# Computing a per-token gate with row sums on VectorE instead of column-tiled matmuls on the matrix engine

## The chip, the cores and the metric

The kernel runs on one core of one Trainium2 chip. The metric is device time in microseconds (us). PE is the matrix engine and PEld its weight loads, DVE is VectorE, ACT is ScalarE, POOL is GpSimd, SP is SyncE, which issues nearly all DMA transfers. The profile covers one execution of the core. Its span is about 1.8 us shorter than the device time of the same execution.

## The reference, cut to what matters

Two attention blocks, A (linear attention) and B (a sliding window of 8 dilated positions), read the same `x` of 2048 tokens by 1024 features. A gate mixes their results:

```python
g = sigmoid((x * gate_w).sum(-1, keepdims=True))      # one number per token
return g * A(x) + (1 - g) * B(x)
```

Most of the projections are 1728 matmuls of 128x128 by 512 columns. The gate is one dot product of 1024 terms for each of 2048 tokens.

## The kernel before: the parts that matter

The kernel is written as a list of operations, each with an engine, an estimated cost, what it reads and writes, and a rank (`prio`, lower goes first). A list scheduler in the kernel, called the planner below, orders each engine's instructions from that. An eviction (the copy of a finished sum out of an accumulator) may have the engine `"any"`; the planner then gives it to ScalarE or VectorE, whichever it expects to be done first. The list fixes the order in which each engine gets its instructions, and SyncE its transfers. An eviction is the copy of a finished sum out of an accumulator.

The first stage computes block B's values, and `x` comes in through transposing loads. The gate stands right behind it, then the keys and queries of B follow:

```python
gwr = SB([128, 8, 32], BF16, "gwr")              # gate_w, 32 copies of each column
P.op("dve", lambda e: e.tensor_copy(gwr[...], gw[:, :, None].to_broadcast([128, 8, 32])), ...)
gbank = main.next()
def gate_fn(e):
    for dc in range(8):
        for u in range(4):                       # four column tiles of 32
            last = e.matmul(gbank.ap()[32 * u:32 * u + 32, :], gwr[:, dc, :], xT[:, dc, u * 512:(u + 1) * 512],
                            start=(dc == 0), stop=(dc == 7), tile_position=(0, 32 * u), skip_group_check=True)
    return last
P.op("pe", gate_fn, 1.75, mode="c", reads=[gwr.all(), xT.all()], writes=[gbank.iv], name="gate")
P.op("act", lambda e: e.activation(gts[:, :], gbank.ap(), ACT.Exp, scale=-1.0), ...)
P.op("sp", ... gt_hbm <- gts[0:128:32, :] ...)   # to DRAM, to turn a row of tokens into partitions
P.op("sp", ... gt <- gt_hbm, rearranged ...)     # and back
# then on VectorE, 128x16 each: gt + 1, g = 1 / gt, gm = 1 - g
...
WARM = 9     # matmuls on zeros at the very start, before data is there
```

Of the kernel before, what the change touches and what calls it, by code (L numbers as in the profile page):

```python
# [6 lines left out]
ACT = mybir.ActivationFunctionType  # L7
ALU = mybir.AluOpType
AX = mybir.AxisListType
BF16 = mybir.dt.bfloat16  # L10
F32 = mybir.dt.float32
I32 = mybir.dt.int32

D = 1024
# [1088 lines left out]
def build_kernel(nc, A_x, A_wqkv, A_wo, B_x, B_wqkv, B_wo, gate_w, out):  # L1103
    del B_x
    S = A_x.shape[1]
    NT = S // 128
    HS = S // 2
    x2 = A_x[0].rearrange("(m e) d -> e m d", e=2)
# [5 lines left out]
    def SB(shape, dtype, name, at=None):  # L1114
        n = SZ[dtype]
        for d in shape[1:]:
            n *= d
        if at is None:
            at = base[0]
            base[0] += (n + 31) // 32 * 32  # L1120
        uid[0] += 1
        h = nc.alloc_sbuf_tensor_at("%s_%d" % (name, uid[0]), list(shape), dtype, offset=at)
        return Tile("S", h, at, list(shape), dtype)
# [29 lines left out]
    vB_hbm = nc.dram_tensor("vB_hbm", [S, D], BF16)  # L1153
    MX = [("M", 0, 1, None)]
    mx_hbm = nc.dram_tensor("mx_hbm", [4, 128], F32)
    GT = [("M", 1, 2, None)]
    gt_hbm = nc.dram_tensor("gt_hbm", [4, 512], F32)

    def hb(p0, p1, half):
        return [("H%d" % half, p0, p1, None)]  # L1160

    xT = SB([128, 8, S], BF16, "xT")
# [8 lines left out]
    KINDS = ((57, (0, 7)), (57, (7, 7)), (56, (7, 8)))  # L1171
    msk = [SB([128, 2, n], BF16, "msk%d" % i) for i, (n, _) in enumerate(KINDS)]
    eps = SB([128, 1], F32, "eps")
    gw = SB([128, 8], BF16, "gw")
    gt = SB([128, NT], F32, "gt")
    g = SB([128, NT], F32, "g")
    gm = SB([128, NT], F32, "gm")
    gwr = SB([128, 8, 32], BF16, "gwr")
    kvbd = SB([128, 8, 128], BF16, "kvbd")
    zbd = SB([128, 8, 128], BF16, "zbd")  # L1180
    kva = SB([128, 8, 33], F32, "kva")
# [5 lines left out]

    ph = base[0]
    vst = Ring([SB([128, 512], BF16, "vst%d" % i) for i in range(8)])
    gts = SB([128, 512], F32, "gts", at=ph)  # L1190
    top_ = base[0]
    base[0] = ph
    Er = Ring([SB([128, 32 * 57], BF16, "E%d" % i) for i in range(2)])
# [8 lines left out]
    ph = base[0]  # L1202
    mx = [SB([128, 1024], BF16, "mx%d" % i, at=ph + 2048 * i) for i in range(2)]
    pk = Ring([SB([128, 1024], BF16, "pk%d" % i) for i in range(2)])
    az = Ring([SB([128, H, 33], BF16, "az%d" % i) for i in range(2)])
    top_ = base[0]
    base[0] = ph
    osb = Ring([SB([128, 1024], BF16, "o%d" % i) for i in range(2)])
# [11 lines left out]
    act = lambda n: 0.19 + n / 1200.0  # L1220
    dps = lambda n: 0.14 + n / 960.0

    def plan(seen):

        P = Prog(nc, nc.alloc_semaphore)
# [66 lines left out]
        def load_x(t, prio):  # L1292
            e_, r = t // 8, t % 8
            return P.op("sp", lambda e: e.dma_start_transpose(xT[:, :, t * 128:(t + 1) * 128], x2[e_, r * 128:(r + 1) * 128, :]),  # L1294
                        1.5, writes=[xT.part((0, 8), (t * 128, (t + 1) * 128))], prio=prio, chan="x%d" % t, lat=1.3)

        def load_w(slot, half, src, c0, prio, d0=0, d1=8, eng="sp", after=()):
            n = d1 - d0
            return P.op(eng, lambda e: e.dma_start(ws[slot][:, d0:d1, half * 512:half * 512 + 512], src[:, d0:d1, c0:c0 + 512]), 0.4 + 0.2 * n,  # L1299
                        writes=[ws[slot].part((d0, d1), (half * 512, half * 512 + 512))], prio=prio, chan="w%d_%d_%d" % (slot, half, d0), lat=0.55 * n, after=after)  # L1300

        def gw_load(e):
            with nc.allow_non_contiguous_dma(reason="tiny gate_w transposed load"):
                return e.dma_start(gw[:, :], gate_w.rearrange("(dc p) -> p dc", p=128))

        load_x(0, 0)
        load_w(0, 0, Bw, 2048, 0.1, 0, 2, "act")
        load_w(0, 0, Bw, 2048, 0.2, 2, 4, "act")
# [3 lines left out]
            load_x(t, 3 + t)  # L1312
        for d in range(0, 8, 2):
            load_w(0, 1, Bw, 2560, 6.1 + 0.1 * d, d, d + 2)
        P.op("sp", gw_load, 0.6, writes=[gw.all()], prio=20, chan="gw", lat=0.5)


        main = Pool(banks[0:7])
# [49 lines left out]
        for t, half in [(4 * b + i, half) for b in range(NT // 4) for half in range(2) for i in range(4)]:  # L1368
# [5 lines left out]
            for d in range(0, 8, step):  # L1374
# [3 lines left out]
                 writes=[hb(t * 128, (t + 1) * 128, half)], chan="vst%d" % vs, lat=0.5, prio=5)  # L1378
# [3 lines left out]
        load_w(0, 1, Aw, 2560, 31)  # L1382


        P.op("dve", lambda e: e.tensor_copy(gwr[:, :, :], gw[:, :, None].to_broadcast([128, 8, 32])), 0.3, reads=[gw.all()], writes=[gwr.all()])
        gbank = main.next()

        def gate_fn(e):
            last = None
            for dc in range(8):  # L1390
                for u in range(4):
                    last = e.matmul(gbank.ap()[32 * u:32 * u + 32, :], gwr[:, dc, :], xT[:, dc, u * 512:(u + 1) * 512], start=(dc == 0), stop=(dc == 7),  # L1392
                                    tile_position=(0, 32 * u), skip_group_check=True)
            return last
        P.op("pe", gate_fn, 1.75, mode="c", reads=[gwr.all(), xT.all()], writes=[gbank.iv], name="gate")
        P.op("act", lambda e: e.activation(gts[:, :], gbank.ap(), ACT.Exp, scale=-1.0), act(512), reads=[gbank.iv], writes=[gts.all()])
        P.op("sp", lambda e: e.dma_start(gt_hbm[:, :], gts[0:128:32, :]), 0.6, reads=[gts.all()], writes=[GT], chan="gto", lat=1.0)

        def gate_in(e):
            with nc.allow_non_contiguous_dma(reason="2048 gates"):  # L1400
                return e.dma_start(gt[:, :], gt_hbm.rearrange("u (k p) -> p (u k)", p=128))
        P.op("sp", gate_in, 0.6, reads=[GT], writes=[gt.all()], chan="gti", lat=6.0)
        P.op("dve", lambda e: e.tensor_scalar(gt[:, :], gt[:, :], 1.0, None, op0=ALU.add), 0.1, reads=[gt.all()], writes=[gt.all()], prio=1e5)
        P.op("dve", lambda e: e.reciprocal(g[:, :], gt[:, :]), 0.25, reads=[gt.all()], writes=[g.all()], prio=1e5)
        P.op("dve", lambda e: e.tensor_scalar(gm[:, :], g[:, :], -1.0, 1.0, op0=ALU.mult, op1=ALU.add), 0.1, reads=[g.all()], writes=[gm.all()], prio=1e5)
# [3 lines left out]
        main = Pool(banks[0:4])  # L1409
# [146 lines left out]
        main = Pool(banks)  # L1556
# [109 lines left out]
        for t in range(NT):  # L1666
# [4 lines left out]
            for f0, f1 in parts:  # L1671
# [3 lines left out]
                def fn(e, t=t, bank=bank, f0=f0, f1=f1):  # L1675
# [6 lines left out]
                    out=o_[:, i0 * 128:i1 * 128].rearrange("p (i s) -> p i s", s=128), in0=bank.ap(0, n).rearrange("p (i s) -> p i s", s=128),  # L1682
                    scalar=gm[:, t:t + 1], in1=tgt[:, i0:i1, c0:c0 + 128], op0=ALU.mult, op1=ALU.add), dps(n),
                    reads=[bank.iv, gm.all(), tgt.part((i0, i1), (c0, c0 + 128))], writes=[o_.part((f0, f1))])
                if t == NT - 1 or f1 == 1024:
                    c = f0 if t == NT - 1 else 0
                    P.op("sp", lambda e, e_=e_, r=r, o_=o_, c=c, f1=f1: e.dma_start(out2[e_, r * 128:(r + 1) * 128, c:f1], o_[:, c:f1]), 0.5,
                         reads=[o_.part((c, f1))], chan="out%d_%d" % (os_, c), lat=1.0)
# [8 lines left out]
    for _ in range(PASSES):  # L1697
        got = plan(seen)
        seen = got[2]
        if best is None or got[0].span < best[0].span:  # L1700
            best = got
    P, flag_op = best[:2]
# [22 lines left out]
def bass_gated_mix__linear_attn_block__sliding_local_dilated__prompt_kernel(nc, A_x, A_wqkv, A_wo, B_x, B_wqkv, B_wo, gate_w, out):  # L1725
    return build_kernel(nc, A_x, A_wqkv, A_wo, B_x, B_wqkv, B_wo, gate_w, out)
# [28 lines left out]
```

## Time and profile before

| | before |
|---|---|
| time, median of 3 runs | 504.89 us (504.59 to 505.67) |
| PE busy | 97% of the span |
| VectorE busy | 53% |
| ScalarE busy | 38% |
| gate matmuls on the chain of waits | 1.84 us |

The page's first part gives busy time (share of the span) and number of instructions for each engine:

```profile
PE 488.5 (97%) x5190; PEld 232.6 (46%) x5257; DVE 264.6 (53%) x456; ACT 192.9 (38%) x335; POOL 6.6 (1%) x30
```

PE is the bottleneck.

The chain of waits, read in order of time: start, duration, what.

```profile
58.71 3.40 PE ps_all L1324 x15
62.11 1.84 PE ps_all L1392 x32
63.95 0.54 PE ps_all L1324 x2
...
127.95 0.63 PE ps_all L1427 x64
...
498.26 0.48 DVE o L1681
```

L1392 is the gate. It is a link of the chain, with other matmuls right ahead of it and right behind it. L1427 is the first group of attention scores, at 127.95 us. The last line is VectorE's last operation. The matmuls around the gate, from the timeline of PE:

```profile
62.05 1.91 PE L1392 MATMUL ps_all<-xT,gwr 128*32 128x512 bf16 x32
63.89 11.40 PE L1324 MATMUL ps_all<-xT,w 128*128 128x512 bf16 x51
```

The gate begins at 62.05 us and the next group at 63.89: 1.84 us.

What the new operations could cost can be read from similar ones. Groups by form on VectorE: names, partitions x elements and types, count, then busy us, mean ns of one.

```profile
L1436 DVE TENSOR_TENSOR E<-E,msk 128x1824 bf16<-128x1824 bf16 x16 | 17.6, 1102 | 13.7 <-ACT E L1433 13.7
L1681 DVE SCALAR_TENSOR_TENSOR o<-ps_all,gm,xT 128x512 bf16<-128x512 f32 x23 | 17.3, 750 | 22.5 <-PE ps_all L1677 22.5
L1681 DVE SCALAR_TENSOR_TENSOR o<-ps_all,gm,xT 128x256 bf16<-128x256 f32 x2 | 1.0, 483 | 0.5 <-PE ps_all L1677 0.4
```

Whether they have room depends on the stretch. The stretches view: length, then busy us (and instructions) of PE, PEld, DVE, ACT and POOL, granted PE clock, DMA share, GB/s.

```profile
52.00:60.00 8.00, 7.95 (x37) 3.61 (x37) 1.87 (x3) 1.19 (x2) 0.00 (x0) 1.00 1.08 345
68.00:76.00 8.00, 7.95 (x38) 3.63 (x38) 4.70 (x8) 1.34 (x3) 0.00 (x0) 1.00 0.78 186
76.00:84.00 8.00, 8.00 (x39) 3.64 (x38) 4.77 (x8) 1.19 (x2) 0.00 (x0) 1.00 0.01 1
100.00:108.00 8.00, 7.95 (x38) 3.64 (x38) 4.89 (x8) 1.19 (x2) 0.00 (x0) 1.00 0.00 0
```

VectorE works under 2 of 8 us from 36 to 60 us, and 3.8 to 5.0 of 8 us while keys and queries are computed. The DMA engines are full until about 72 us and idle afterwards.

### The profile page before, as it was taken

Reading aid. Unit: us, or ns where it says so; the run is one execution under the profiler, and the core shown is the slowest. Engines: PE = TensorE matmul, PEld = TensorE weight load, DVE = VectorE, ACT = ScalarE, POOL = GpSimd, SP = SyncE. Lnnn points to the kernel's source line nnn. Section 1 sums busy time; section 2 is a strip of 40 time slices with the busy share of each in tenths; the row PEclk is TensorE's granted clock in tenths of the full one; section 3 lists DMA queues with packets and bytes.
Section 4 is the critical chain, followed back from the end, with each engine's and each line's share of the span. In section 5 each row is a group of like instructions: output and inputs, shape, how many; then the busy total and the mean of one; then the engine's idle time right before and its main releaser. Section 6 shows DMA issues by size and latency. Waiting matters only on the chain.

```text
span 502.5 us, 11582 instructions
## 1 busy us (share of the span) xinstructions
PE 488.5 (97%) x5190; PEld 232.6 (46%) x5257; DVE 264.6 (53%) x456; ACT 192.9 (38%) x335; POOL 6.6 (1%) x30
## 2 busy tenths in 40 slices
PE   8999999999999999999999999999999999999996
PEld 2444444444454444544544545444444444444443
DVE  3112235556667676454555464678776563234443
ACT  1111111111354454655554555479864543100000
POOL 5000000000000000000000000000000000000000
PEclk9999999999999999999999999999999999999999
DMA  8999990000024060100010100500000000011222
GB/s 222 207 204 314 353 270 1 1 0 1 12 86 139 22 198 27 34 23 23 23 39 21 33 1 3 170 0 1 0 2 0 2 0 1 1 43 64 83 78 73
DMA packets 47410, 34.92 MB, mean 69 GB/s; under 512 B 22261, under 2 KB 43125, under 8 KB 47354
## 3 DMA queue, kind: packets, MB, share of 16 engines
q1 hardware_dynamic: 46810, 33.59, 23.6%
q8 instruction: 43, 0.70, 0.6%
q10 hardware_dynamic: 544, 0.52, 0.4%
q14 instruction: 13, 0.11, 0.1%
HBM read 21.51 MB, written 8.40 MB: 60 GB/s over the span
## 4 chain that ended last, share of the span: by engine, by line
PE 95%; issue 2%; DMA 1%; ACT 1%; SPq 0%; DVE 0%
PE ps_all L1324 76%; PE ps_all L1677 11%; PE ps_all L1427 2%; PE ps_all L1447 2%; PE ps_all L1602 1%; PE ps_all L1452 1%; PE ps_all L1523 1%; DMA xT<-in_A_x_dram 1%; PE ps_all L1580 1%; ACT ra L1604 0%; PE ps_all L1392 0%; SPq L1294 0%; SPq L1299 0%; ACT e L1333 0%; ACT ra L1605 0%
## 5 line engine op out<-in xcount | busy, mean ns | idle before, releaser
L1324 PE MATMUL ps_all<-w,xT 128*128 128x512 bf16 x922 | 207.8, 379 | 5.6 <-issue 4.0
L1324 PE MATMUL ps_all<-xT,w 128*128 128x512 bf16 x747 | 169.2, 379 | 2.5 <-issue 1.9
L1324 PEld LDWEIGHTS ps_all<-w,xT 128*128 128x128 bf16 x960 | 91.3, 98 | 110.3 <-issue 1.7
L1324 PEld LDWEIGHTS ps_all<-xT,w 128*128 128x128 bf16 x768 | 73.9, 98 | 88.8 <-ACT ra L1604 0.6
L1677 PE MATMUL ps_all<-w,qT 128*128 128x512 bf16 (+1 forms) x259 | 55.2, 373 | 0.3
L1677 PEld LDWEIGHTS ps_all<-w,qT 128*128 128x128 bf16 x264 | 25.8, 98 | 29.7
L1335 DVE TENSOR_SCALAR e<-e 128x512 bf16<-128x512 bf16 x64 | 18.4, 291 | 38.9 <-ACT e L1331 25.3
L1355 DVE CAST vst<-ps_all 128x512 bf16<-128x512 f32 x15 | 10.4, 691 | 42.7 <-PE ps_all L1324 42.7
L1433 ACT ACTIVATE E<-ps_all 128x1824 bf16<-128x1824 f32 (+1 forms) x18 | 30.4, 1687 | 3.1 <-PE ps_all L1427 2.0
L1331 ACT ACTIVATE e<-ps_all 128x512 bf16<-128x512 f32 x32 | 19.1, 597 | 31.6 <-PE ps_all L1324 30.8
L1333 ACT ACTIVATE e<-ps_all 128x512 bf16<-128x512 f32 x32 | 19.2, 601 | 29.3 <-PE ps_all L1324 27.8
L1681 DVE SCALAR_TENSOR_TENSOR o<-ps_all,gm,xT 128x512 bf16<-128x512 f32 (+1 forms) x25 | 18.2, 729 | 23.0 <-PE ps_all L1677 22.8
L1280 DVE TENSOR_TENSOR mx<-mx,kT 128x1024 bf16<-128x1024 bf16 x32 | 20.7, 688 | 16.9 <-ACT kT L1356 16.8
L1280 DVE TENSOR_TENSOR mx<-mx,qT 128x1024 bf16<-128x1024 bf16 x32 | 20.7, 688 | 16.7 <-ACT qT L1359 16.6
L1356 ACT ACTIVATE vst<-ps_all 128x512 bf16<-128x512 f32 x17 | 10.1, 597 | 47.8 <-PE ps_all L1324 47.8
L1436 DVE TENSOR_TENSOR E<-E,msk 128x1824 bf16<-128x1824 bf16 (+1 forms) x18 | 19.8, 1100 | 14.5 <-ACT E L1433 14.5
L1462 DVE TENSOR_TENSOR qT<-ps_all,L 128x456 bf16<-128x456 f32 (+1 forms) x36 | 21.1, 624 | 7.7 <-ACT L L1461 7.7
L1359 ACT ACTIVATE qT<-ps_all 128x512 bf16<-128x512 f32 x15 | 9.0, 597 | 37.0 <-PE ps_all L1324 37.0
L1337 DVE SCALAR_TENSOR_TENSOR pk<-ps_all,e 128x512 bf16<-128x512 f32 x32 | 22.0, 688 | 0.8
L1604 ACT ACTIVATE ra<-ps_all,eps 128x512 f32<-128x512 f32 x32 | 21.5, 688 | 2.2 <-PE ps_all L1602 2.0
L1356 ACT ACTIVATE az<-ps_all 128x512 bf16<-128x512 f32 x19 | 11.4, 600 | 27.6 <-PE ps_all L1324 27.6
L1356 ACT ACTIVATE kT<-ps_all 128x512 bf16<-128x512 f32 x14 | 8.4, 597 | 35.5 <-PE ps_all L1324 35.5
(77 smaller groups left out, 336.5 us busy)
## 6 DMA issues: line engine op xcount, KB each, us to landing
w<-in_A_wqkv_dram SPq DMA_DIRECT2D x6, 1024.0 KB, 8.2
v<-vB_hbm SPq DMA_DIRECT2D x36, 128.0 KB, 2.6
vB_hbm<-vst SPq DMA_DIRECT2D x32, 128.0 KB, 4.9
w<-in_B_wqkv_dram SPq DMA_DIRECT2D x4, 1024.0 KB, 8.3
out_dram<-o SPq DMA_DIRECT2D x15, 256.0 KB, 2.0
w<-in_A_wo_dram SPq DMA_DIRECT2D x2, 1024.0 KB, 5.6
w<-in_B_wo_dram SPq DMA_DIRECT2D x2, 1024.0 KB, 6.5
w<-in_B_wqkv_dram SPq DMA_DIRECT2D x6, 256.0 KB, 4.1
```

The costliest lines, as they stand in the source:

```text
L1280: P.op("dve", lambda e, m=m, op=op: e.tensor_tensor(m[:, 0:n], m[:, 0:n], src, op), 0.08 + n / 1920.0, reads=[m.all(), reg], writes=[m.all()],
L1324: last = e.matmul(bank.ap(), lhs(dc), rhs(dc), start=(dc == 0), stop=(dc == 7))
L1331: P.op("act", lambda e: e.activation(e_[:, :], bank.ap(), ACT.Exp), act(512), reads=[bank.iv], writes=[e_.all()])
L1333: P.op("act", lambda e: e.activation(e_[:, :], bank.ap(), ACT.Exp, accum_out=qe[:, col:col + 1]), act(512) + 0.1, reads=[bank.iv], writes= ...
L1335: P.op("dve", lambda e: e.tensor_scalar(e_[:, :], e_[:, :], 1.0, 1e-6, op0=ALU.min, op1=ALU.add), 0.25, reads=[e_.all()], writes=[e_.all()])
L1337: P.op("dve", lambda e: e.scalar_tensor_tensor(out=dst, in0=bank.ap(), scalar=0.0, in1=e_[:, :], op0=ALU.max, op1=ALU.add), dps(512), read ...
L1356: fa = lambda e: e.activation(dst, src(), ACT.Copy)
L1433: P.op("act", lambda e: e.activation(E[:, 0:32 * nq].rearrange("p (j q) -> p j q", j=4), ps[:, 4:8, 0:8 * nq], ACT.Exp), act(32 * nq), rea ...
L1436: P.op("dve", lambda e: e.tensor_tensor(ev(), ev(), m[:, :, :].rearrange("p r q -> p (r q)")[:, None, :].to_broadcast([128, 16, 2 * nq]), ...
L1462: P.op("dve", lambda e, L=L, pb=pb, g=g: e.tensor_tensor(qT[:, 4 * g:4 * g + 4, t0 + qs:t0 + qs + 2 * nq].rearrange("p c (h q) -> p h c q" ...
L1604: P.op("act", lambda e: e.activation(R[:, :], db.ap(), ACT.Ln, bias=eps[:, :]), act(512), reads=[db.iv, eps.all()], writes=[R.all()])
L1677: last = e.matmul(bank.ap(0, f1 - f0), qT[:, dc, t * 128:(t + 1) * 128], ws[3][:, dc, f0:f1], start=(dc == 0), stop=(dc == 7))
```

## The change

Intent: take the gate off the bottleneck. `x` is loaded a second time, untransposed, 128 tokens at a time. VectorE multiplies each tile by `gate_w` (broadcast to all partitions) and sums along the row with the accumulating output of `scalar_tensor_tensor`. The result has tokens on partitions already, so the trip through DRAM goes too. The two landing buffers `xn` share memory with the `az` tiles, which are used only later. The diff, cut to its core:

```diff
-        P.op("dve", lambda e: e.tensor_copy(gwr[:, :, :], gw[:, :, None].to_broadcast([128, 8, 32])), ...)
-        gbank = main.next()
-        def gate_fn(e): ...                            # the 32 matmuls shown above
-        P.op("pe", gate_fn, 1.75, mode="c", ..., name="gate")
-        P.op("act", lambda e: e.activation(gts[:, :], gbank.ap(), ACT.Exp, scale=-1.0), ...)
-        P.op("sp", lambda e: e.dma_start(gt_hbm[:, :], gts[0:128:32, :]), ...)
-        P.op("sp", gate_in, ...)
+    xn = Ring([SB([128, 1024], BF16, "xn%d" % i, at=az.t[i].lo) for i in range(2)])
...
-        P.op("sp", gw_load, 0.6, writes=[gw.all()], prio=20, chan="gw", lat=0.5)
+        P.op("sp", lambda e: e.dma_start(gwb[:, :], gate_w[None, :].to_broadcast([128, D])), 0.6, writes=[gwb.all()], prio=29, ...)
...
+        for t in range(NT):                            # NT = 16
+            xt, xs_ = xn.next()
+            P.op("sp", lambda e, t=t, xt=xt: e.dma_start(xt[:, :], x2[t // 8, (t % 8) * 128:(t % 8) * 128 + 128, :]), 0.6, writes=[xt.all()], ...)
+            P.op("dve", lambda e, t=t, xt=xt: e.scalar_tensor_tensor(out=xt[:, :], in0=xt[:, :], scalar=1.0, in1=gwb[:, :],
+                 op0=ALU.mult, op1=ALU.mult, accum_out=gt[:, t:t + 1]), dps(1024), reads=[xt.all(), gwb.all()],
+                 writes=[xt.all(), gt.part((t, t + 1))], prio=1000 + len(P.ops) + 80)
+        P.op("act", lambda e: e.activation(gt[:, :], gt[:, :], ACT.Exp, scale=-1.0), act(NT), ...)
```

More of the change, by code (lines that the diff above doesn't have):

```diff
@@ L1155, in build_kernel @@
     mx_hbm = nc.dram_tensor("mx_hbm", [4, 128], F32)
-    GT = [("M", 1, 2, None)]
-    gt_hbm = nc.dram_tensor("gt_hbm", [4, 512], F32)
     def hb(p0, p1, half):
@@ L1173, in build_kernel @@
     eps = SB([128, 1], F32, "eps")
-    gw = SB([128, 8], BF16, "gw")
+    gwb = SB([128, 1024], BF16, "gwb")
     gt = SB([128, NT], F32, "gt")
@@ L1177, in build_kernel @@
     gm = SB([128, NT], F32, "gm")
-    gwr = SB([128, 8, 32], BF16, "gwr")
     kvbd = SB([128, 8, 128], BF16, "kvbd")
@@ L1189, in build_kernel @@
     vst = Ring([SB([128, 512], BF16, "vst%d" % i) for i in range(8)])
-    gts = SB([128, 512], F32, "gts", at=ph)
     top_ = base[0]
@@ L1300, in load_w @@
                         writes=[ws[slot].part((d0, d1), (half * 512, half * 512 + 512))], prio=prio, chan="w%d_%d_%d" % (slot, half, d0), lat=0.55 * n, after=after)
-        def gw_load(e):
-            with nc.allow_non_contiguous_dma(reason="tiny gate_w transposed load"):
-                return e.dma_start(gw[:, :], gate_w.rearrange("(dc p) -> p dc", p=128))
         load_x(0, 0)
@@ L1314, in plan @@
             load_w(0, 1, Bw, 2560, 6.1 + 0.1 * d, d, d + 2)
-        P.op("sp", gw_load, 0.6, writes=[gw.all()], prio=20, chan="gw", lat=0.5)
+        P.op("sp", lambda e: e.dma_start(gwb[:, :], gate_w[None, :].to_broadcast([128, D])), 0.6, writes=[gwb.all()], prio=29, chan="gw", lat=0.8)
         main = Pool(banks[0:7])
@@ L1382, in plan @@
         load_w(0, 1, Aw, 2560, 31)
-        P.op("dve", lambda e: e.tensor_copy(gwr[:, :, :], gw[:, :, None].to_broadcast([128, 8, 32])), 0.3, reads=[gw.all()], writes=[gwr.all()])
-        gbank = main.next()
-        def gate_fn(e):
-            last = None
-            for dc in range(8):
-                for u in range(4):
-                    last = e.matmul(gbank.ap()[32 * u:32 * u + 32, :], gwr[:, dc, :], xT[:, dc, u * 512:(u + 1) * 512], start=(dc == 0), stop=(dc == 7),
-                                    tile_position=(0, 32 * u), skip_group_check=True)
-            return last
-        P.op("pe", gate_fn, 1.75, mode="c", reads=[gwr.all(), xT.all()], writes=[gbank.iv], name="gate")
-        P.op("act", lambda e: e.activation(gts[:, :], gbank.ap(), ACT.Exp, scale=-1.0), act(512), reads=[gbank.iv], writes=[gts.all()])
-        P.op("sp", lambda e: e.dma_start(gt_hbm[:, :], gts[0:128:32, :]), 0.6, reads=[gts.all()], writes=[GT], chan="gto", lat=1.0)
-        def gate_in(e):
-            with nc.allow_non_contiguous_dma(reason="2048 gates"):
-                return e.dma_start(gt[:, :], gt_hbm.rearrange("u (k p) -> p (u k)", p=128))
-        P.op("sp", gate_in, 0.6, reads=[GT], writes=[gt.all()], chan="gti", lat=6.0)
+        for t in range(NT):
+            xt, xs_ = xn.next()
+            P.op("sp", lambda e, t=t, xt=xt: e.dma_start(xt[:, :], x2[t // 8, (t % 8) * 128:(t % 8) * 128 + 128, :]), 0.6, writes=[xt.all()], chan="xn%d" % xs_, lat=1.0)
+            P.op("dve", lambda e, t=t, xt=xt: e.scalar_tensor_tensor(out=xt[:, :], in0=xt[:, :], scalar=1.0, in1=gwb[:, :], op0=ALU.mult, op1=ALU.mult,
+                                                                      accum_out=gt[:, t:t + 1]), dps(1024), reads=[xt.all(), gwb.all()], writes=[xt.all(), gt.part((t, t + 1))],
+                 prio=1000 + len(P.ops) + 80)
+        P.op("act", lambda e: e.activation(gt[:, :], gt[:, :], ACT.Exp, scale=-1.0), act(NT), reads=[gt.all()], writes=[gt.all()], prio=1000 + len(P.ops) + 100)
         P.op("dve", lambda e: e.tensor_scalar(gt[:, :], gt[:, :], 1.0, None, op0=ALU.add), 0.1, reads=[gt.all()], writes=[gt.all()], prio=1e5)
```

## The prediction

> **What bounds the kernel.** The matrix engine: the page's first part has it busy 488.5 of 502.5 us (97%), the chain of waits puts 95% of the span on it, and the granted clock is 1.00 nearly everywhere. VectorE is busy 53%, ScalarE 38%. A saving counts only if it shortens PE's list; an addition costs only if it makes PE wait.
>
> **What goes.**
> - The 32 gate matmuls. The chain has them as one piece, 62.11 to 63.95 us: 1.84 us, nothing overlapped. (A full group of 8 costs 1.73 us.) The PE timeline shows no further gap around them; weight loads idle 0.4 us on either side, hidden. All 1.84 us are on the chain.
> - The ScalarE eviction (0.60 us), the VectorE copy into gwr (0.29 us), and the DRAM round trip (issued at 67.5, back at 76.8 us). All off the chain: VectorE finishes the gate at 95 us and it is first used at 365.5 us.
>
> **What comes.**
> - 16 VectorE ops of 128x1024 with summed output. From the trace: two-input ops with a PSUM source take 751 ns for 512 columns and 482 for 256, so 1.05 ns a column; the 16-bit tensor-tensor ops (1824 columns 1100 ns, 1024 columns 688 ns) leave a fixed 0.16 us. Estimate 1.24 us, if no packed mode applies. The Trainium skill, "VectorE: DVE Perf Modes", section "Two Vector instructions with no wait between them", says an op that also writes its accumulator is two instructions; the trace has no example on this engine. I allow 0.1 us: 1.3 us each, 21 us in all, VectorE busy 264.6 to about 285 us.
> - 16 loads of 256 KB (4.2 MB) and a 256 KB broadcast, with two landing buffers. The stretches view has the DMA engines full from 4 to 72 us and idle from 76 to 130. At the 350 to 380 GB/s seen there, 4.4 MB are 12 us of queue, so the full stretch ends nearer 84 us.
>
> **Does it reach PE?** I expect not. From 45 to 62 us VectorE works 0.69 us in each 3.45; from 64 to 130 us some 2.0, leaving 1.5 us, enough for one new op per 3.45 us. Even all 16 there end by 125 us, before the attention stage (74% busy). Evictions may slip by one op, 1.3 us; the four accumulators of that stage leave about 3 x 1.73 - 0.7 = 4.5 us before PE must wait. Weights fetched while DMA is full are needed late: the key and query halves issued by 48 us at 64 and 92 us, later ones near 195. The hazards are in-order queues: VectorE waiting for a late row load holds evictions behind it, and SyncE waiting for a buffer holds other loads. Before, VectorE already waited 1.7 us for gw and PE did not notice.
>
> **Sum.** 504.9 - 1.84 = 503.0 us. The instruction order is replanned for all engines, so unrelated stalls (the 3 us one at 345 us on ScalarE) can move by a microsecond either way.
>
> Predicted: 503.0 us, 8 in 10 between 501.6 and 505.0. Faster by over 2%: 0.01; within 2%: 0.95; slower by over 2%: 0.04.
>
> **What would show it.** PE busy down by 1.9 us and no column-tiled gate group in the chain; 16 new VectorE ops near 1.3 us, done before 128 us; VectorE busy up some 20 us; PE's waits on VectorE still near nothing; DMA full until about 84 us.
>
> **What would make it wrong.** PE idle between 45 and 130 us released by an eviction: a row load landed late in front of VectorE. Or vB stores and weights pushed back until PE waits on weights at 64 or 92 us. Or a worse order in the attention stage, unrelated to the gate.

## The result and the profile after

The changed kernel took 502.34 us (median of 4 runs, 502.29 to 502.62) against 504.74 us (4 runs, 504.45 to 505.67) for the kernel before. The ratio is 0.9953, with a 95% interval of 0.9939 to 0.9967.

The saving of the medians, 2.40 us, is larger than the 1.84 us that the gate matmuls took. Either something else was saved too, or the 0.56 us are scatter. That became the question for the experiments.

First the page:

```profile
PE 493.8 (99%) x5225; PEld 231.6 (46%) x5225; DVE 278.7 (56%) x482; ACT 195.4 (39%) x340; POOL 6.9 (1%) x30
```

PE's busy time went *up*, from 488.5 to 493.8 us. This is no extra work. This trace has all its matmul records (5225 matmuls, 5225 weight loads), the one before lacked 67. The weight loads tell the truth: 5257 to 5225, exactly the 32 of the gate. The order of the weight loads in the two traces says the same: it is identical but for the one gate group. The replanning, which the prediction feared, did not touch PE.

The chain and the timeline of PE, at the places shown before:

```profile
126.20 0.63 PE ps_all L1409 x64
...
496.58 0.48 DVE o L1663
```

```profile
8.29 54.02 PE L1317 MATMUL ps_all<-w,xT 128*128 128x512 bf16 x248 [0.19 <-DMA xT<-in_A_x_dram]
62.15 13.12 PE L1317 MATMUL ps_all<-xT,w 128*128 128x512 bf16 x60
```

The next stage begins at 62.15 us, where the gate began before. From there to the last VectorE operation it is 496.58 - 62.15 = 434.43 us; before it was 498.26 - 63.89 = 434.37 us. So from these marks on, the two traces differ by the gate and by nothing else.

The new operations, and the queue that feeds them (an engine, what it waited for, us in total, times, longest):

```profile
L1381 DVE SCALAR_TENSOR_TENSOR xn<-xn,gwb 128x1024 bf16<-128x1024 bf16 x16 | 18.9, 1221 | 0.0
L1381 DVE DVE_READ_ACCUMULATOR xn<-xn,gwb 128x1 f32 x16 | 1.3, 84 | 0.0
```

```profile
SPq L1380 <- DVE xn L1381: 41.1, 12, 17.2
```

```profile
52.00:60.00 8.00, 8.00 (x39) 3.62 (x38) 4.45 (x7) 1.19 (x2) 0.00 (x0) 1.00 1.03 338
76.00:84.00 8.00, 8.00 (x39) 3.63 (x38) 4.09 (x7) 1.79 (x3) 0.00 (x0) 1.00 0.18 34
100.00:108.00 8.00, 8.00 (x39) 3.63 (x38) 7.08 (x13) 2.39 (x4) 0.00 (x0) 1.00 0.27 86
116.00:124.00 8.00, 8.00 (x39) 3.62 (x37) 7.84 (x15) 2.37 (x5) 0.48 (x2) 1.00 0.20 66
```

VectorE is nearly full between 92 and 124 us (7.08 and 7.84 of 8 us shown here), while PE has no gap. Two of the sums come early, at 56 us; the other 14 run from 89 to 122.5 us. SyncE waits 41.1 us for a landing buffer, so that twelve of the sixteen loads are issued after 90 us, past the full stretch.

### The profile page after: what moved, and what is told of

It reads as the page before. It is cut to its first block, busy times and chain, and to the rows that moved or that the text cites. A ratio compares the mean times of both kernels' runs of the same rounds, so it can differ in the third digit from the quotient of the medians. Undisturbed runs are those within 1.5% of the kernel's fastest.

```text
span 500.9 us, 11634 instructions
## 1 busy us (share of the span) xinstructions
PE 493.8 (99%) x5225; PEld 231.6 (46%) x5225; DVE 278.7 (56%) x482; ACT 195.4 (39%) x340; POOL 6.9 (1%) x30
## 4 chain that ended last, share of the span: by engine, by line
PE 96%; SPq 2%; DMA 1%; ACT 1%; issue 0%; DVE 0%
PE ps_all L1317 76%; PE ps_all L1659 11%; PE ps_all L1409 2%; PE ps_all L1429 2%; SPq L1291 1%; PE ps_all L1584 1%; PE ps_all L1434 1%; PE ps_all L1505 1%; DMA w<-in_B_wqkv_dram 1%; PE ps_all L1562 1%; SPq L1296 1%; ACT ra L1586 0%; ACT e L1326 0%; ACT ra L1587 0%; DVE o L1663 0%
## 5 line engine op out<-in xcount | busy, mean ns | idle before, releaser
L1317 PE MATMUL ps_all<-w,xT 128*128 128x512 bf16 x960 | 214.2, 380 | 1.4 <-DMA xT<-in_A_x_dram 1.2
L1317 PE MATMUL ps_all<-xT,w 128*128 128x512 bf16 x768 | 172.4, 380 | 0.1
L1349 ACT ACTIVATE kT<-ps_all 128x512 bf16<-128x512 f32 x17 | 10.1, 597 | 38.7 <-PE ps_all L1317 38.7
L1352 ACT ACTIVATE qT<-ps_all 128x512 bf16<-128x512 f32 x17 | 10.1, 597 | 34.2 <-PE ps_all L1317 34.2
L1351 DVE TENSOR_SCALAR xT<-ps_all,g 128x512 bf16<-128x512 f32 x15 | 11.3, 750 | 19.9 <-PE ps_all L1317 19.9
```

Source lines behind the costliest of these rows:

```text
L1317: last = e.matmul(bank.ap(), lhs(dc), rhs(dc), start=(dc == 0), stop=(dc == 7))
L1349: fa = lambda e: e.activation(dst, src(), ACT.Copy)
```

## The experiments

The kernel before was timed beside each call, so medians are compared inside a call. "gate4", for example, means the experiment of that name.

### Is it the gate alone? r_after, no_gate, both, gate4 (one call; before: 504.43 us, 11 runs, 503.74 to 505.98)

**r_after**: the changed kernel unchanged, timed again.

> The changed kernel once more, beside the kernel before, for a tight difference. The first timing gave a saving of 2.40 us where the traced gate matmuls are 1.84 us. Theory A (only the matrix engine's list counts, the rest of the 2.4 is scatter between runs): 1.8 to 2.0 us less than before, about 502.7 if before is 504.7. Theory B (something else in the removed path, such as the DRAM round trip or the eviction, costs about half a microsecond too): 2.3 to 2.5 us less.

Measured: 502.63 us (6 runs, 502.19 to 503.92), ratio 0.9959 (0.9943 to 0.9976). This time the medians differ by 1.80 us.

**no_gate**: no gate at all.

```diff
-        (gwr copy, gate matmuls, eviction to gts, DRAM round trip, load of gw)
+        P.op("pool", lambda e: e.memset(gt[:, :], 1.0), 0.1, writes=[gt.all()])
```

> The kernel before with no gate at all: no gate matmuls, no eviction, no round trip, no row loads, no VectorE sums; the gate is a constant, so the result is wrong on purpose. The matrix engine's order is otherwise identical. If the new VectorE work and the row loads are free, this takes the same time as the changed kernel, within 0.3 us. If they cost something hidden, this is faster than the changed kernel by that much.

Measured: 502.24 us (6 runs, 501.72 to 503.45), wrong (relative error 0.039). It is 0.39 us under r_after, slightly outside the 0.3 us expected, with each kernel's own runs scattering by 1.7 us. The traces decide better; see the table below.

**both**: the changed kernel plus the old gate, which writes into a tile that nobody reads.

```diff
+        (gwr copy, gate matmuls, eviction to gts, DRAM round trip as before,)
+        P.op("sp", ... e.dma_start(gt2[:, :], gt_hbm...) ..., writes=[gt2.all()], ...)
```

> The changed kernel with the old gate added again: matmuls, eviction and round trip into a tile that nothing reads. Result right. If the VectorE gate is free and the whole difference lies in the removed path, this takes the time of before within 0.3 us (about 504.7). If the new work costs X, it takes before plus X.

Measured: 504.41 us (6 runs, 503.90 to 505.77), ratio 0.9990 (0.9976 to 1.0005). That is the time of before: with the matmuls back, the saving is gone, and the VectorE gate beside them costs nothing visible.

**gate4**: the 32 matmuls four times over.

```diff
-            for dc in range(8):
+            for dc in [d for _ in range(4) for d in range(8)]:
```

> The kernel before with its 32 gate matmuls run four times over in one piece, same result; eviction and round trip once, the switch into and out of the column-tiled form once. Theory A: before plus 3 x 1.84 = 5.5 us, about 510.2, and the removal in r_after is worth one such term, 1.84 us, plus whatever one switch costs (0.1 us). Theory B: plus 5.5 us here too, but 2.4 us for the removal, because the extra is outside the matmuls.

Measured: 509.62 us (5 runs, 509.30 to 510.74), ratio 1.0094. The medians differ by 5.19 us, 1.73 us for each extra set. The timeline of PE in gate4:

```profile
6.39 57.28 PE L1324 MATMUL ps_all<-w,xT 128*128 128x512 bf16 x256 [1.12 <-DMA xT<-in_A_x_dram]
63.60 7.09 PE L1392 MATMUL ps_all<-xT,gwr 128*32 128x512 bf16 x128
70.62 4.71 PE L1324 MATMUL ps_all<-xT,w 128*128 128x512 bf16 x21
```

Four sets take 70.62 - 63.60 = 7.02 us, one takes 1.84 us. So an extra set is (7.02 - 1.84) / 3 = 1.73 us, and 0.11 us of the single one are paid once. These lines show a second such loss, ahead of the gate. A matmul's record lasts 0.38 us, so the last ordinary matmul begins at 6.39 + 57.28 - 0.38 = 63.29 us and the gate at 63.60. That is 0.31 us, where ordinary ones begin 0.216 us apart: 0.09 us are lost on entering the column-tiled form (four matmuls side by side, each in 32 columns of the array). After the gate the gap is 0.31 us again (63.60 + 7.09 - 0.38 = 70.31 to 70.62), which is the 0.11 us, paid on leaving.

So 1.84 us, counted from the first gate matmul, is a little short. From the last ordinary matmul before the gate to the first one after it, the traces of before and both have 2.152 us on average; those of after, r_after and no_gate have 0.216 us at this place. The gate costs PE 1.94 us.

All traces can be cut at the same two places. Read from the timeline of PE and the end of the chain:

| run | values of B done | gate | rest, to the start of the last VectorE operation |
|---|---|---|---|
| before | 62.05 | 1.84 | 434.37 |
| after | 62.15 | none | 434.43 |
| r_after | 62.24 | none | 434.32 |
| no_gate | 62.09 | none | 434.30 |
| both | 63.55 | 1.84 | 434.37 |
| gate4 | 63.60 | 7.02 | 434.32 |

The last column agrees within 0.13 us, with a gate on VectorE, on PE, on both or on neither. The VectorE work and the loads are free, and so were the eviction and the round trip. Everything else that moves is in the first column, ahead of the gate. (The 0.09 us for entering the gate are in it too.)

### What scatters in the first 62 us? before_w13 and after_w13 (before in this call: 504.07 us, 11 runs, 503.58 to 505.37)

The two traces with a late first column, both and gate4, are also the slowest run of their kernel. Their first real matmuls are slow. Weight loads of both, in order of time:

```profile
6.85 0.15 PEld L1328 LDWEIGHTS ps_all<-w,xT 128*128 128x128 bf16 x1 [0.27 <-issue]
7.28 0.15 PEld L1328 LDWEIGHTS ps_all<-w,xT 128*128 128x128 bf16 x1 [0.28 <-issue]
...
9.84 0.15 PEld L1328 LDWEIGHTS ps_all<-w,xT 128*128 128x128 bf16 x1 [0.28 <-issue]
10.14 13.91 PEld L1328 LDWEIGHTS ps_all<-w,xT 128*128 128x128 bf16 x65 [0.15 <-issue]
```

They are 0.43 us apart until about 10 us and 13.91 / 65 = 0.214 us afterwards. In the trace of before the real matmuls go at the fast pace from the first one. So they do in r_after, although they begin there at the same time as in the run both and after the same pause of 1.2 us behind the warming matmuls:

```profile
6.44 0.99 PEld L1317 LDWEIGHTS ps_all<-w,xT 128*128 128x128 bf16 x6 [2.08 <-issue]
```

The Trainium skill, "TensorE: Matmul & The Clock Gate", section "Part 1: The HAM clock gate (the "warmup" mystery)", describes this: a cold array runs at half rate until it has been busy for a window of some 3.4 us, the window is free-running, and so the number of cold matmuls varies from run to run (426.7 and 215.7 ns apart at 512 columns). The trace agrees with both rates. To test it, the 9 warming matmuls became 13.

```diff
-    WARM = 9
+    WARM = 13
```

> The kernel before with 13 warming matmuls in place of 9; matrix order otherwise the same. In the traces so far all scatter lies ahead of 62 us: in the two profiled runs that were slow (both, gate4) the first 9 or so real matmuls started 427 ns apart after a pause of about 1.2 us behind the warming ones, in the others 216 ns apart. Theory A (scatter is this cold start): the slow runs vanish, all runs within about 0.4 us, near the fastest of before (503.7 to 504.4), no real matmuls at 427 ns. Theory B (scatter is the landing of the first loads): scatter of 1 to 2 us stays.

> The changed kernel with 13 warming matmuls. Theory A: 1.84 us (1.7 to 2.0) under before_w13, with both kernels' scatter small, so the change is worth the traced gate and no more; 501.9 to 502.4. Theory B of the first call (something besides the gate matmuls also saved): 2.3 us or more under before_w13.

Measured: before_w13 504.50 us (5 runs, 504.23 to 504.62), after_w13 502.13 us (5 runs, 502.06 to 502.34). The scatter fell to 0.39 and 0.28 us. This alone proves little: 6 of the 42 runs of before lie above 505.3 us, the others below 505.0, and at that rate (an estimate) ten runs without a slow one come up by chance in one case of five; stt3, with 9, also scattered by only 0.55 us in five runs. The trace of after_w13 says more:

```profile
5.92 0.15 PEld L1356 LDWEIGHTS ps_all<-warm 128*128 128x128 bf16 x1 [0.28 <-issue]
6.35 0.15 PEld L1317 LDWEIGHTS ps_all<-w,xT 128*128 128x128 bf16 x1 [0.28 <-issue]
6.78 7.26 PEld L1317 LDWEIGHTS ps_all<-w,xT 128*128 128x128 bf16 x34 [0.28 <-issue]
```

A weight load runs ahead of its matmul; the first real matmul starts at 6.77 us. So the pace was slow through all 13 warming matmuls and fast from the real ones on. Nine would have ended at 5.3 us, before it turned. That the two traced slow runs owe their delay to slow first matmuls is shown; that 13 warming matmuls cure it is likely, but not shown. Another part of the expectation failed: before_w13 is not near the fastest runs of before, its median lies 0.43 us above that of before (ratio 1.0006, 0.9994 to 1.0019, so no clear difference).

The two medians differ by 2.37 us and the means by 2.24 us, which is on the side of Theory B. But the two traces do not show a second saving. Before_w13 starts its gate at 62.05 us and its last VectorE operation at 498.21; after_w13 starts the next stage at 62.07 and ends at 496.38. That is 436.16 against 434.31 us, a difference of 1.85 us. The spans of the two profiled executions differ by 502.5 - 500.6 = 1.9 us and their times by 504.32 - 502.32 = 2.00 us.

So the timed saving came out as 2.40, 1.80 and 2.37 us, and both against r_after gives 1.78 us. All 42 runs of before have a mean of 504.50 us, the 10 runs of the changed kernel 502.60 us: 1.90 us. The traced saving is 1.84 to 1.85 us from the first gate matmul on, and 1.94 us with the entry. A further half microsecond is not in any trace. But one execution of each kernel was traced, and why the untraced ones of the w13 pair differ by more is open. Builds whose traces agree differ about as much: the medians of no_gate (502.24) and stt3 (502.20) lie 0.4 us under that of r_after.

### How much VectorE work is free? stt3, stt6, stt6_own

**stt3**: each sum three times, two of them into a scratch tile.

```diff
+            for _ in range(2):
+                P.op("dve", ... scalar_tensor_tensor(out=scr[:, :], in0=xt[:, :], ..., accum_out=gx[:, t:t + 1]), ...)
```

> The changed kernel with each row sum done three times (twice into a scratch tile): 32 more VectorE ops of 1.3 us, 42 us more. Result right. VectorE would need more than the 66 us between 60 and 126 us, so the surplus moves into the attention stage and the planner orders that stage otherwise. If VectorE work is free wherever it fits: under 1 us more than the changed kernel. If the order of evictions breaks when the stage is full: 2 us or more, with matrix idle or a different order after 126 us.

Measured: 502.20 us (5 runs, 501.85 to 502.40), ratio 0.9960: the changed kernel's time, with 32 more operations. The page says where they went:

```profile
PE 486.3 (97%) x5159; PEld 232.0 (46%) x5225; DVE 305.2 (61%) x527; ACT 206.0 (41%) x359; POOL 6.9 (1%) x30
```

VectorE grew by 305.2 - 278.7 = 26.5 us and ScalarE by 10.6 us, together about the 32 x 1.15 = 37 us that the new operations take back to back. Evictions moved to ScalarE, which had room, and the last sum slid to 143 us, into the attention stage. (PE's order did change from there on, without cost. The 486.3 us of PE are missing records again: 5159 matmuls, 5225 weight loads.)

**stt6**: each sum six times, 80 extra operations (before in its call: 504.32 us, 9 runs).

> Each row sum six times over, 80 more VectorE ops of 1.3 us, 104 us more. In stt3 42 us more cost nothing: VectorE grew by 27 us only, and ScalarE by 11, because the planner moved evictions there. The planner here orders the attention stage otherwise (checked before the run). If two engines that can stand in for one another take any load that fits: within 0.5 us of the changed kernel. If 104 us is past what the stages from 60 to 330 us can hold: 2 us or more.

Measured: 547.29 us (4 runs, 547.01 to 547.53), ratio 1.0852. The free room ended: 43 us over before. The waits of PE, longest first in total:

```profile
PE ps_all L1435 <- DVE E L1424: 14.6, 4, 3.8
PE ps_all L1415 <- DVE qT L1450: 13.5, 4, 4.9
PE ps_all L1319 <- ACT az L1351: 10.4, 1, 10.4
```

```profile
126.00:180.00 54.00, 53.89 (x279) 24.33 (x266) 52.82 (x87) 19.27 (x31) 0.00 (x0) 1.00 0.34 112
180.00:234.00 54.00, 14.16 (x593) 8.50 (x594) 53.62 (x89) 16.68 (x25) 0.47 (x2) 0.57 0.09 26
```

VectorE is full from 126 to 234 us. While projections last, PE does them ahead of time and stays busy. From 180 us it needs attention results that stand behind the sums in VectorE's list (the masked scores `E`, the quotient `qT`), or behind work that the sums have pushed back, and it works 14.16 of 54 us. The last sum ends at 196.8 us. After it VectorE does mostly running maxima of keys and queries (`mx`), until 233 us; in the changed kernel these were done by 184 us. The mean granted clock from 180 to 234 us is 0.57.

**stt6_own**: the third wait, on `az`, suggested another cause: `az` shares memory with the landing buffers, so it cannot be written before the last sum. Here the buffers have other memory.

```diff
-    xn = Ring([SB([128, 1024], BF16, "xn%d" % i, at=az.t[i].lo) for i in range(2)])
+    xn = Ring([SB([128, 1024], BF16, "xn%d" % i, at=pq0.lo + 2048 * i) for i in range(2)])
```

> stt6 with the two landing buffers of the rows moved from the az tiles to pq0, which is free until 326 us; nothing else changed, matrix order identical to stt6 (checked before the run). In stt6 the matrix engine stood still from 180 to 190 us because az could not be written before the last sum had read its row (10.4 us in the waits), and afterwards waited for VectorE. If the shared memory is the cause of the first part: 8 to 11 us under stt6, about 537 us. If VectorE's backlog alone sets the time: no change, within 1 us of 547.3 us, the 10 us turning up as a wait for a VectorE result instead.

Measured: 547.39 us (4 runs, 546.79 to 547.54; before 504.44 us, 7 runs). Nothing was gained. The waits of PE:

```profile
PE ps_all L1435 <- DVE E L1424: 27.5, 4, 16.3
PE ps_all L1415 <- DVE qT L1450: 13.4, 4, 4.9
```

The wait on `az` is gone, and PE stands still for 16.3 us at the next thing that VectorE owes it. The shared memory was where the backlog showed, not what made the kernel slow.

The amount of work need not be the limit either. From 60 to 330 us VectorE is idle for some 100 us in the changed kernel (270 us less 169.6 busy), the 80 extra sums take 80 x 1.15 = 92 us, and `g` is first used at 363.8 us. In the planner's order, sums and maxima stand ahead of results that PE needs. A later rank for the sums was not tried, so stt6 gives the limit of this order, not of the engine.

### Does the place matter? early, early_load, high_sum

**early**: loads between the transposing loads of `x` from the start, and sums ahead of evictions. **early_load** and **high_sum** do one half each (same call as stt6).

```diff
-  ... gwb load ..., prio=29          # early, early_load
+  ... gwb load ..., prio=3
-  ... xn load ...                    # early, early_load
+  ... xn load ..., prio=3.5 + t
-  ... sum ..., prio=1000 + len(P.ops) + 80     # early, high_sum
+  ... sum ..., prio=900
```

> The changed kernel with the row loads and the broadcast put between the transposing loads of x from the start, and the sums put ahead of the evictions; matrix order the same. They now run in the stretch where the DMA engines are full (4 to 72 us) and the first one stands before the second tile of x. If position does not matter because the evictions have slack: within 0.5 us of the changed kernel. If it does: the matrix engine waits for x in the first 60 us, slower by 2 us or more, and all of it before 62 us.

> The other half of early: the row loads and the broadcast stand between the transposing loads of x from the start, the sums keep their low rank. Matrix order the same. If the loads at the start are the cause, this loses what early lost, 4 to 7 us over the changed kernel, in waits of the matrix engine for x and weights before 25 us. If the rank of the sums is the cause: within 0.5 us of the changed kernel.

> One half of early: the row loads stay where the changed kernel has them, only the sums go ahead of the evictions in VectorE's order. Matrix order the same. If early lost its 6.7 us to evictions held behind sums that wait for late rows, this is slower too, by 1 us or more. If early lost it to the loads at the start, this takes the changed kernel's time within 0.3 us.

Measured: early 508.97 us (6 runs, 507.15 to 509.07; before 504.07), early_load 507.35 us (5 runs, 506.88 to 507.50; before 504.32), high_sum 502.60 us (5 runs, 502.20 to 503.67; before 504.32). With late loads the rank of the sums costs nothing against the changed kernel's 502.63; the place of the loads costs 4.7 us. The timeline of PE in early_load:

```profile
5.80 2.03 PE L1317 MATMUL ps_all<-w,xT 128*128 128x512 bf16 x8 [0.53 <-DMA xT<-in_A_x_dram]
11.37 8.33 PE L1317 MATMUL ps_all<-w,xT 128*128 128x512 bf16 x30 [3.54 <-DMA xT<-in_A_x_dram]
20.05 47.23 PE L1317 MATMUL ps_all<-w,xT 128*128 128x512 bf16 x218 [0.35 <-DMA w<-in_B_wqkv_dram]
67.12 8.15 PE L1317 MATMUL ps_all<-xT,w 128*128 128x512 bf16 x37
```

PE waits 3.54 us for the second tile of `x`, which came behind the row loads, then has a mean granted clock of 0.66 from 11 to 16 us (1.00 in the changed kernel), and reaches the next stage at 67.12 us in place of 62.15. In early, VectorE itself waited 7.9 us for late rows, in front of evictions, yet PE waited for DMA only. Still, early is 1.6 us slower than early_load. Its trace has a second wait, of 1.98 us for weights (0.35 in early_load). Whether the rank of the sums brought that about is open. The first stage has seven accumulators to write to (`Pool(banks[0:7])`), one new one each 1.73 us, which would explain why the evictions had time; no run varied their number.

## Why the prediction was right

- **The saving is the gate's time on PE, 1.84 us.** Right in the mechanism, and 0.09 us short. The prediction saw no further gap around the gate, but entering it costs that much, so PE saves 1.94 us. Predicted 503.0 us, measured 502.34, inside 501.6 to 505.0. That range also holds the time before (504.74), so the number alone would prove little; the traces and experiments do. Most of the 0.66 us is scatter of the early medians: from all runs, 504.50 - 1.94 = 502.56 us against a mean of 502.60 us. no_gate, both and gate4 show that nothing else of the old path was on the chain. That the replanning might shift unrelated stalls did not come true: PE's order was identical.
- **Cost of the new operations, 1.24 + 0.1 us.** Right: 1.22 us. The second instruction of which "VectorE: DVE Perf Modes", section "Two Vector instructions with no wait between them", told is there, an accumulator read of 0.084 us. Back to back the pair takes 1.15 us from start to start, for the records overlap.
- **VectorE busy up some 20 us.** Too high: 14.1 us. The overlap makes it 16 x 1.15 = 18.4 us, the copy into gwr (0.29 us) is gone, and five evictions of keys and queries moved to ScalarE (17 + 17 there against 14 + 15 before), 5 x 0.69 = 3.4 us. That leaves 14.7 us. The prediction had taken the evictions' engines as fixed.
- **Just enough room, all done before 125 us.** The end was right (122.5 us), the limit was not. stt3 put in 32 more operations, 37 us, at no cost in time. The margin was mis-sized because it counted only VectorE's idle time in one stage, not the exchange with ScalarE nor the next stage.
- **DMA full until about 84 us.** Wrong, and harmless: the share falls to 0.18 in the stretch from 76 us on. Only four row loads were issued in the full stretch, as two landing buffers made SyncE wait 41.1 us for VectorE; the other twelve came after 90 us.
- **PE busy down by 1.9 us, to be seen on the page.** A bad test: missing records moved that number by more than 5 us the other way. The start of the next stage and the count of weight loads were the good ones.
- **What would make it wrong.** Rows late in front of VectorE made PE wait for no eviction, even when provoked (early). Loads pushing back the first `x` and weights did (early_load), before 25 us and not at 64 or 92 us as named.

No version is shown to beat the changed kernel. after_w13 has the lowest median of a right result with the plain change, 502.13 us, and no slow run in five, but its gain over 502.34 to 502.63 us is within what medians of one kernel differ by.

## What to carry to other kernels

On a kernel with one engine 97% busy, a move of work off that engine is worth the traced time of the piece on the chain, with the gaps at both of its ends (count from the last start before it to the first start after it). Work put on an engine with slack is free until a result that the full engine needs stands behind it; then it is suddenly not, as 32 against 80 extra operations showed. Compare two traces by marks that both have (the start of the same stage, the last operation), not by busy sums, which lose records. A wait names the first thing that was late, so take it away in an experiment before calling it the cause.

## What the Trainium skill lacked or had wrong

- "VectorE: DVE Perf Modes", section "The perf-mode tier table (the rule you actually need)", has no row for `scalar_tensor_tensor`. With two bf16 inputs in SBUF and a summed output, 1024 columns took 1.22 us here, where a bf16 `tensor_tensor` of 1024 columns took 0.69 us: by the times, no packed mode.
- The same page, section "Two Vector instructions with no wait between them", says that an accumulating op is two instructions, which the trace confirms, but gives no duration: the read took 84 ns, and pairs follow each other every 1.15 us.
- "TensorE: Matmul & The Clock Gate", section "Part 1: The HAM clock gate (the "warmup" mystery)", says that cold counts vary from run to run, which these traces confirm. For benchmarks the page's section "Why this matters for your kernels" advises 4 us or more of matmuls first. That was not always enough here: the fast pace began 2.9 us after the first warming matmul in before_w13 and 5.5 us after it in after_w13. In the run both, 4.02 us of warming and a pause of 1.2 us were followed by slow matmuls.
- "TensorEngine Tiling (Array Packing)", section "Key Properties", says that changing the tiling mode drains the engine and gives no time: here going in cost 0.09 us and coming out 0.11 us.
